# Attention and two dense products on one core: outputs and next scores as one piece in three PSUM banks

## The chip, the cores and the metric

The kernel runs on one core of a Trainium2 chip. The metric is the device time of one execution in microseconds (us). The kernel before takes 915.24 us, the median of three runs (914.27 to 915.32).

The core has a matrix engine (PE, whose weight loads are shown as PEld), a vector engine (DVE), a scalar engine (ACT), a third elementwise engine (POOL), and a queue (SP) that only issues DMAs here. Each engine works through its own list of instructions in order, and semaphores make one wait for another. PE writes its results to PSUM, a memory of eight banks; a bank holds 512 float32 values in each of 128 partitions. DVE and ACT read PSUM.

## The reference

For 8 batches of 8 heads, 576 positions and head size 64, masked attention is computed. Heads 0 to 3 look at the 32 latest positions, heads 4 to 7 at every fourth of the 128 latest. The result, 4608 rows of 512, goes through two dense products with an ELU between them:

```python
scores = np.where(masks, q @ k.T / sqrt(64), -1e9)
attn = softmax(scores)                       # per row, sum + 1e-9
x = (attn @ v) as (4608, 512)
h = x @ w_in                                 # (4608, 2048)
g = np.where(h > 0, h, np.exp(np.minimum(h, 0)) - 1)
out = g @ w_out                              # (4608, 512)
```

All is float32. The kernel gets near that accuracy with a faster matmul type (fp32r): it splits a value into a high part and a low part and forms three products (high times high, high times low, low times high).

## The kernel before, in words

**Tiling.** The 4608 rows are worked in nine chunks of 512 (`NCH`, index c), the 2048 hidden columns in 16 tiles of 128 (`NF`, index f). For each chunk and hidden tile, `product1` (L285) forms the first product in one PSUM bank `h_ps` with 12 matmuls; `elu` (L302) turns it into `gh` and `gl`; and `gemm2` (L318) adds 12 matmuls into four banks `o_ps`, the chunk's output. In the first 12 hidden tiles of chunk 0 the weights aren't split yet: there are four matmuls in full float32 in place of each 12.

**Order on PE.** All matmuls keep the order in which the program lists them (`mm`, L81). In the main loop (L403) hidden tile f runs its first product, then a step of attention if one is due, then the second product of tile f - 2 (`flush(LAG)`). After a chunk's last second product, `store` (L326) copies the four output banks with ACT and SP stores them.

**Order on the other engines.** The order on ACT, DVE, POOL and SP is made by a planner, which simulates the kernel's time and takes instructions as they become ready, those with the least slack first. `tc.issue_after(ins)` ties what is listed in the block behind `ins` on the same engine. So the order on ACT and DVE can't be read in the code; it can be read in the trace.

**Attention.** A pair is two heads; a batch has four pairs (`NPAIR`). The first batch goes through `first_attention` (L193) before chunk 0. During chunk c (0 to 6), `batch_attention(c + 1)` (L332) works the next batch in eight steps, spread over the hidden tiles (L432: f = 1, 3, 5, 7, 9, 11, 13, 14): scores of pair 0, scores of 1, outputs of 0, scores of 2, outputs of 1, scores of 3, outputs of 2, outputs of 3. Chunks 7 and 8 have no attention beside them.

A scores step (`attention` up to its first `yield`, L242 to L263) puts 36 small matmuls, 72 instructions, into the two banks `a_ps0` and `a_ps1` (`banks`, L189), 384 columns each. DVE adds the mask (L252), takes the row maxima (L253, L254); ACT takes 12 exponentials with their sums (L256); the sums are inverted, POOL multiplies (L183, in batch 1 DVE does), and DVE transposes into `pt` (L262). An outputs step (`outputs`, L163) has 12 matmuls of 96 columns, 24 instructions, into the same two banks, and two ACT copies of 288 columns into `x32` (L173, L176). At the start of a chunk `split_x` (L271) splits 512 rows of `x32` into `xh` and `xl`.

**PSUM in the main loop.** Four banks `o_ps`, two `a_ps`, two `h_ps` (the pool `ps_h`, bufs=2, L373): eight in all. A bank `h_ps` is read by ACT (L304, the exponential) and by DVE (L311, the maximum with zero); the next but one first product may write it after both.

**Loads.** `load_pair` (L147) has SP load the q, k and v of a pair into buffers of which there are two each. The weights come through `load_w` (L84); some rooms `early` (L67) serve the first batch before a weight tile takes them.

Of the kernel before, what the change touches and what calls it, by code (L numbers as in the profile page):

```python
# [10 lines left out]
F32 = mybir.dt.float32  # L11
# [12 lines left out]
P = 128  # L24
G = 32
# [21 lines left out]
def body(ctx: ExitStack, tc: tile.TileContext, q, k, v, masks, w_in, w_out, out):  # L47
# [141 lines left out]
    def banks():  # L189

        return [ps_a.tile([P, TC], F32, name=f"a_ps{i}") for i in range(2)]

    def first_attention(hp, loaded):  # L193

        dil = hp >= NPAIR // 2
        qt, kt, vt = loaded
        if hp >= 2:
            sm = early[2 * (hp - 2) + 1][:QB, 2 * NU * D:2 * NU * (D + 2 * G)].rearrange("p (u j) -> p u j", u=2 * NU)
        else:
            sm = ap.tile([QB, 2 * NU, 2 * G], F32, name="sm")  # L200
        mx = ap.tile([QB, 2 * NU], F32, name="nmx", bufs=4)
        sums = ap.tile([QB, 2 * NU], F32, name="sums", bufs=4)
        s_ps = ps_f.tile([P, 2, TC], F32, name="ab"[hp % 2])[:QB, :, :NU * 2 * G]
        for h in range(2):
            mm(s_ps[:, h, :], ones_sb, mask_sb[:, int(dil), :], start=True, stop=False)
        scores([s_ps[:, h, :] for h in range(2)], qt, kt, False)
        yield
        s4 = s_ps.rearrange("p h (n j) -> p h n j", n=NU)
        mx4 = mx.rearrange("p (h n) -> p h n", h=2)
        inorder(nc.vector.tensor_reduce(out=mx4, in_=s4, op=ALU.max, axis=mybir.AxisListType.X))  # L210
# [12 lines left out]

        t_ps = (ps_c, ps_f)[hp % 2].tile([P, 2, TC], F32, name="ca"[hp % 2])
        for n in range(NU):
            for h in range(2):
                o = n % NA * QB
                mm(t_ps[h * 2 * G:(h + 1) * 2 * G, n // NA, o:o + QB], sm[:, h * NU + n, :], ident, start=True, stop=True)
        t4 = t_ps[:, :, :NA * QB].rearrange("p i (n q) -> p i n q", n=NA)
        for h in range(2):  # L230
            to = tr[:, h * NU:(h + 1) * NU, :].rearrange("p (i n) q -> p i n q", i=2)
            for c, r, m in ((0, 0, 2), (1, 0, 1), (1, 1, 1), (2, 0, 2)):
                cs, ks, rs = slice(c * G, (c + 1) * G), slice((c + r) * G, (c + r + m) * G), slice((h * 2 + r) * G, (h * 2 + r + m) * G)
                if hp == NPAIR - 1:
                    inorder(nc.vector.tensor_copy(out=to[ks, :, :, cs], in_=t4[rs, :, :, cs]))
                else:
                    inorder(nc.scalar.copy(out=to[ks, :, :, cs], in_=t4[rs, :, :, cs]))
            yield
        a_ps = ps_f.tile([P, 2, TC], F32, name="db"[hp % 2])
        yield outputs(0, hp, [(a_ps[:, i, :], i * NA, (i + 1) * NA) for i in range(NU // NA)], vt, tr, inorder)  # L240

    def attention(b, hp, loaded):  # L242

        dil = hp >= NPAIR // 2
        qt, kt, vt = loaded
        sm = ap.tile([QB, 2 * NU, 2 * G], F32, name="sm")
        nmx = ap.tile([QB, 2 * NU], F32, name="nmx", bufs=4)
        sums = ap.tile([QB, 2 * NU], F32, name="sums", bufs=4)
        s_ps = [s[:QB, :NU * 2 * G] for s in banks()]
        scores(s_ps, qt, kt, True)  # L250
        for h in range(2):
            nc.vector.tensor_tensor(out=sm[:, h * NU:(h + 1) * NU, :].rearrange("p n j -> p (n j)"), in0=s_ps[h], in1=mask_sb[:, int(dil), :], op=ALU.add)  # L252
        nc.vector.tensor_reduce(out=nmx, in_=sm, op=ALU.max, axis=mybir.AxisListType.X)  # L253
        nc.vector.tensor_scalar(out=nmx, in0=nmx, scalar1=-0.125, scalar2=None, op0=ALU.mult)  # L254
        for u in range(2 * NU):
            nc.scalar.activation(out=sm[:, u, :], in_=sm[:, u, :], func=AF.Exp, bias=nmx[:, u:u + 1], scale=0.125, accum_out=sums[:, u:u + 1])  # L256
        normalise(nc.vector if b < 2 else nc.gpsimd, sm, sums, lambda ins: ins)
        tr = transposed()
        for c in range(GU):
            for r in range(2):  # L260
                ks, cs, rs = slice((c + r) * G, (c + r + 1) * G), slice(c * G, (c + 1) * G), slice(r * G, (r + 1) * G)
                nc.vector.transpose(out=tr[ks, :, cs], in_=sm[cs, :, rs])  # L262
        yield  # L263
        outputs(b, hp, [(a, i * NA, (i + 1) * NA) for i, a in enumerate(banks())], vt, tr)
        yield

    xh, xl = [None] * NC, [None] * NC

    hidden, below = [], []

    def split_x(c):  # L271
        for hp in range(NC):
# [11 lines left out]

    def product1(c, f):  # L285

        h_ps = ps_h.tile([P, TC], F32, name="h_ps")
        i = 2 * f
        if c == 0 and f < F0:
            terms = [(full[i], x32[0][:, n, :TC], n) for n in range(NC)]  # L290
        else:
            terms = [(wh[i], x[n], n) for n in range(NC) for x in (xh, xl)] + [(wl[i], xh[n], n) for n in range(NC)]
        for t, (w, x, n) in enumerate(terms):
            mm(h_ps, w[:, n * P:(n + 1) * P], x, start=t == 0, stop=t == len(terms) - 1)
            yield h_ps
# [5 lines left out]

    def elu(h_ps, first):  # L302
        e = fp.tile([P, TC], F32, name="e", bufs=3)
        nc.scalar.activation(out=e, in_=h_ps, func=AF.Exp)  # L304
        if first:
            below.append(nc.scalar.activation(out=e, in_=e, func=AF.Relu, scale=-1.0, bias=1.0).ins)
            g = fp.tile([P, TC], F32, name="gh", bufs=3)
            hidden.append(nc.vector.scalar_tensor_tensor(out=g, in0=h_ps, scalar=0.0, in1=e, op0=ALU.max, op1=ALU.subtract).ins)
            return g, None
        nc.vector.tensor_scalar(out=e, in0=e, scalar1=1.0, scalar2=-1.0, op0=ALU.min, op1=ALU.add)  # L310
        hidden.append(nc.vector.scalar_tensor_tensor(out=e, in0=h_ps, scalar=0.0, in1=e, op0=ALU.max, op1=ALU.add).ins)  # L311
        gh = fp.tile([P, TC], F32R, name="gh", bufs=3)
        gl = fp.tile([P, TC], F32R, name="gl", bufs=2)
        nc.scalar.copy(out=gh, in_=e)  # L314
        nc.vector.tensor_tensor(out=gl, in0=e, in1=gh.bitcast(F32), op=ALU.subtract)  # L315
        return gh, gl
# [15 lines left out]
    def batch_attention(b):  # L332

        x32[b] = xp.tile([P, NPAIR, S], F32, name="x32", bufs=2)

        old = None
        for hp in range(NPAIR):
            it = attention(b, hp, loaded.pop((b, hp)))
            next(it)
            nxt = b * NPAIR + hp + 1  # L340
            if nxt < B * NPAIR:
                loaded[divmod(nxt, NPAIR)] = load_pair(*divmod(nxt, NPAIR))
            yield
            if old is not None:
                next(old)
                yield
            old = it
        next(old)
        yield

    STEPS = 2 * NPAIR
    loaded = {}
    rooms = [room(0, hp) for hp in range(NPAIR)]

    for what in "m0 qk0 qk1 qk2 qk3 v0 v1 w0 v2 v3".split():
# [13 lines left out]
    for what in "S0 S1 M0 M1 S2 P0 M2 T0 U0 S3 P1 P2 A0 T1 M3 U1 O0 T2 U2 P3 B0 O1 T3 U3 O2 G0 G1 O3 G2 A1 C0 D1".split():  # L369
        i = int(what[1])  # L370
        if what == "G0":
            ps_second.close()
            ps_h = ctx.enter_context(tc.tile_pool(name="ps_h", bufs=2, space=bass.MemoryType.PSUM, side="right"))  # L373
            first = product1(0, 0)
        if what[0] == "A":
            inorder(magnitude(i))
# [10 lines left out]
    loaded[1, 0] = load_pair(1, 0)  # L387
    for j in range(NR - NE, NR + 2):
        load_w(j)
    split = 0  # L390
    pend = []
    o_of = {}

# [9 lines left out]
    for c in range(NCH):  # L403
# [2 lines left out]
                split_x(c)  # L406
        elif c > 1:
            split_x(c)
        att = batch_attention(c + 1) if c + 1 < B else iter(())
        emitted = 0  # L410
        for f in range(NF):
            while c == 0 and ready < min(NF, f + AHEAD):
# [13 lines left out]
            while c == 1 and split < min(K0, f + 2):  # L426
# [2 lines left out]
                    split_w(split)  # L429
                split += 1  # L430
            pend.append((c, f, elu(gemm1(c, f), c == 0 and f < F0)))
            while emitted < (f + 1) * STEPS // (NF - 1):  # L432
                emitted += 1
                if c == 0 and emitted <= 2:
# [65 lines left out]
```

## Time and profile before

| what | value |
|---|---|
| median of the three runs | 915.24 us (914.27 to 915.32) |
| the profiled execution, its own time | 914.69 us |
| its span, first to last instruction | 912.9 us |
| mean granted PE clock | 0.994 of full |
| PE busy | 895.5 us, 98% |
| PEld busy | 694.8 us, 76% |
| DVE busy | 530.6 us, 58% |
| ACT busy | 392.3 us, 43% |
| POOL busy | 45.0 us, 5% |
| idle time of PE that the wait table lists | 13.3 us, all before 131 us |

How to read it: rows of the timeline show start, duration, engine, line of the code, operation, `output<-inputs`, shapes and a count (x4) where equal neighbours are merged; in brackets stands idle time before them and what ended it. Large matmuls are pipelined, so their rows overlap (0.39 us long, one every 0.23 us); the pace is read from the starts. L82 is the helper through which every matmul goes, so matmuls are told apart by their tiles: `h_ps` first product, `o_ps` second product, `a_ps<-kt,qt` scores, `a_ps<-pt,vt` outputs. In a row of groups, `| 17.2, 584 |` is busy us and the mean of one in ns. In a row of stretches, `97.52 (x770)` is busy us and instructions of one engine.

### The profile page before, as it was taken

Reading aid. Unit: us, or ns where it says so; the run is one execution under the profiler, and the core shown is the slowest. Engines: PE = TensorE matmul, PEld = TensorE weight load, DVE = VectorE, ACT = ScalarE, POOL = GpSimd, SP = SyncE. Lnnn points to the kernel's source line nnn. Section 1 sums busy time; section 2 is a strip of 40 time slices with the busy share of each in tenths; the row PEclk is TensorE's granted clock in tenths of the full one; section 3 lists DMA queues with packets and bytes.
Section 4 is the critical chain, followed back from the end, with each engine's and each line's share of the span. In section 5 each row is a group of like instructions: output and inputs, shape, how many; then the busy total and the mean of one; then the engine's idle time right before and its main releaser. Section 6 shows DMA issues by size and latency. Waiting matters only on the chain.

```text
span 912.9 us, 15990 instructions
## 1 busy us (share of the span) xinstructions
PE 895.5 (98%) x6536; PEld 694.8 (76%) x6536; DVE 530.6 (58%) x926; ACT 392.3 (43%) x1185; POOL 45.0 (5%) x36
## 2 busy tenths in 40 slices
PE   6899989999999999999999999999999999999998
PEld 5444458888878887888888787888788888888886
DVE  5999998765465556554565556655655533343332
ACT  4763593543354434444543345433543432233222
POOL 2000000100001000000000001000000000000000
PEclk8999999999999999999999999999999999999999
DMA  9963102111031113101211112011300010001001
GB/s 350 404 233 121 44 19 81 54 46 34 29 101 45 45 36 101 43 23 60 73 45 45 46 46 88 29 45 36 101 19 18 1 47 1 0 1 47 1 1 46
DMA packets 23802, 59.40 MB, mean 65 GB/s; under 512 B 2640, under 2 KB 2736, under 8 KB 23728
## 3 DMA queue, kind: packets, MB, share of 16 engines
q1 hardware_dynamic: 23728, 58.37, 19.2%
q8 instruction: 51, 0.84, 0.4%
q14 instruction: 23, 0.19, 0.1%
HBM read 48.92 MB, written 9.44 MB: 64 GB/s over the span
## 4 chain that ended last, share of the span: by engine, by line
PE 87%; ACT 5%; DVE 4%; DMA 3%; issue 1%; SPq 0%; ACTq 0%; DVEq 0%
PE o_ps L82 41%; PE h_ps L82 40%; PE a_ps L82 5%; ACT sm L256 3%; DMA r<-w_out 2%; DMA r<-w_in 1%; ACT r L131 1%; DMA kt<-k 1%; DVE nmx L253 1%; DVE sm L252 1%; ACT e L304 0%; DVE a L115 0%; DVE a L113 0%; DVE e L311 0%; ACT o L329 0%
## 5 line engine op out<-in xcount | busy, mean ns | idle before, releaser
L82 PE MATMUL o_ps<-a,gh 128*128 128x512 f32 x576 | 207.3, 429 | 0.0
L82 PE MATMUL o_ps<-r,gh 128*128 128x512 f32 x576 | 195.3, 398 | 0.4
L82 PE MATMUL h_ps<-xh,r 128*128 128x512 f32 x512 | 183.5, 393 | 3.0 <-ACT x L173 3.0
L304 ACT ACTIVATE e<-h_ps 128x512 f32<-128x512 f32 x144 | 85.5, 594 | 228.6 <-PE h_ps L82 228.5
L314 ACT CAST gh<-e 128x512 fp32r<-128x512 f32 x132 | 82.0, 621 | 194.2 <-DVE e L311 194.1
L310 DVE TENSOR_SCALAR e<-e 128x512 f32<-128x512 f32 x132 | 63.5, 481 | 163.2 <-ACT e L304 162.1
L82 PE MATMUL h_ps<-xh,a 128*128 128x512 f32 x480 | 147.7, 389 | 0.0
L82 PE MATMUL h_ps<-xl,r 128*128 128x512 f32 x368 | 143.9, 391 | 0.0
L82 PE MATMUL o_ps<-r,gl 128*128 128x512 f32 x368 | 143.5, 390 | 0.0
L82 PEld LDWEIGHTS o_ps<-a,gh 128*128 128x128 f32 x576 | 106.5, 188 | 39.4 <-issue 19.6
L315 DVE TENSOR_TENSOR gl<-e,gh 128x512 fp32r<-128x512 f32 x132 | 91.2, 691 | 77.4 <-PE o_ps L82 60.1
L82 PEld LDWEIGHTS o_ps<-r,gh 128*128 128x128 f32 x576 | 106.6, 188 | 26.9 <-ACT o L329 2.5
L256 ACT ACTIVATE sm<-sm,nmx 96x64 f32<-96x64 f32 x336 | 112.1, 335 | 33.0 <-DVE nmx L254 32.6
L82 PEld LDWEIGHTS h_ps<-xh,r 128*128 128x128 f32 x512 | 96.7, 189 | 24.5 <-ACT x L173 3.8
L82 PEld LDWEIGHTS h_ps<-xh,a 128*128 128x128 f32 x480 | 90.1, 188 | 18.7
L262 DVE STREAM_TRANSPOSE pt<-sm 32x384 f32<-32x384 f32 x168 | 95.5, 568 | 12.9 <-POOL sm L183 11.0
L311 DVE SCALAR_TENSOR_TENSOR e<-h_ps,e 128x512 f32<-128x512 f32 x132 | 91.1, 690 | 4.0
L82 PEld LDWEIGHTS h_ps<-xl,r 128*128 128x128 f32 x368 | 69.6, 189 | 15.0 <-issue 0.5
L82 PEld LDWEIGHTS o_ps<-r,gl 128*128 128x128 f32 x368 | 69.1, 188 | 15.1
L183 POOL TENSOR_TENSOR sm<-sm,sums 96x768 f32<-96x768 f32 x25 | 40.4, 1616 | 654.8 <-ACT e L304 298.3
L256 ACT ACTIVATION_READ_ACCUMULATOR sm<-sm,nmx 96x1 f32 x336 | 62.9, 187 | 0.0
L82 PE MATMUL o_ps<-a,gl 128*128 128x512 f32 x160 | 62.5, 391 | 0.0
(90 smaller groups left out, 697.3 us busy)
## 6 DMA issues: line engine op xcount, KB each, us to landing
vt<-v SPq DMA_DIRECT2D x30, 384.0 KB, 3.0
kt<-k SPq DMA_DIRECT2D x30, 304.0 KB, 4.1
qt<-q SPq DMA_DIRECT2D x30, 288.0 KB, 3.2
r<-w_in SPq DMA_DIRECT2D x16, 512.0 KB, 7.7
r<-w_out SPq DMA_DIRECT2D x16, 512.0 KB, 7.8
out<-o SPq DMA_DIRECT2D x32, 256.0 KB, 3.4
out<-xl SPq DMA_DIRECT2D x4, 256.0 KB, 2.1
r<-v SPq DMA_DIRECT2D x2, 384.0 KB, 9.1
```

What stands on the lines that cost most here:

```text
L82: inorder(nc.tensor.matmul(*args, **kw))
L131: nc.scalar.copy(out=h, in_=full2[k])
L183: return keep(eng.tensor_tensor(out=sm, in0=sm, in1=sums.unsqueeze(2).broadcast_to([QB, 2 * NU, 2 * G]), op=ALU.mult))
L252: nc.vector.tensor_tensor(out=sm[:, h * NU:(h + 1) * NU, :].rearrange("p n j -> p (n j)"), in0=s_ps[h], in1=mask_sb[:, int(dil), :], op=AL ...
L253: nc.vector.tensor_reduce(out=nmx, in_=sm, op=ALU.max, axis=mybir.AxisListType.X)
L256: nc.scalar.activation(out=sm[:, u, :], in_=sm[:, u, :], func=AF.Exp, bias=nmx[:, u:u + 1], scale=0.125, accum_out=sums[:, u:u + 1])
L262: nc.vector.transpose(out=tr[ks, :, cs], in_=sm[cs, :, rs])
L304: nc.scalar.activation(out=e, in_=h_ps, func=AF.Exp)
L310: nc.vector.tensor_scalar(out=e, in0=e, scalar1=1.0, scalar2=-1.0, op0=ALU.min, op1=ALU.add)
L311: hidden.append(nc.vector.scalar_tensor_tensor(out=e, in0=h_ps, scalar=0.0, in1=e, op0=ALU.max, op1=ALU.add).ins)
L314: nc.scalar.copy(out=gh, in_=e)
L315: nc.vector.tensor_tensor(out=gl, in0=e, in1=gh.bitcast(F32), op=ALU.subtract)
```

## The change

In chunk 0 nothing moves: its batch keeps the steps of before (the function that makes them is now `probabilities`, which ends with the transposed probabilities; the outputs are called beside it). In chunks 1 to 6 attention goes in pieces (`piece`): the outputs of one pair and the scores of the next, with nothing between them on PE. They stand behind the first product of f = 0, 4, 7, 11 and 14 in chunk 1 and f = 2, 6, 10 and 14 in chunks 2 to 6. Chunk 1's first piece is scores alone; its last one holds the scores of the next batch's first pair; chunk 6's last piece is outputs alone.

A piece uses three banks: `a_ps0`, `a_ps1` and `h1`. The last 96 columns of the outputs go to `a_ps0`, behind the room of its scores, the other 480 to `h1`. ACT copies both out. The scores of the next pair go to the first 384 columns of `a_ps0` and `a_ps1`.

`h1` was one of the two banks of the first product. In chunks 1 to 6 the first product has only `h0`; in chunks 0, 7 and 8 it still alternates. After chunk 0's first 12 hidden tiles, ACT first copies the first product into SBUF (`h`, one buffer), and the exponential and DVE's maximum read the copy.

Of the 12 exponentials of a pair, six are listed with the piece, six and all that follows them after the next hidden tile's copy (`issue_after(freed[-1])`). The loads of the next pair are listed after the transposes. The buffer `sm` becomes a single one; in the first batch, pair 1's `sm` goes to a room of `early`.

```diff
-        if hp >= 2:
-            sm = early[2 * (hp - 2) + 1][:QB, 2 * NU * D:2 * NU * (D + 2 * G)]...
+        if hp > 0:
+            room, o = (early[0], WINDOW + 2 * S) if hp == 1 else (early[2 * (hp - 2) + 1], 2 * NU * D)
+            sm = room[:QB, o:o + 2 * NU * 2 * G].rearrange("p (u j) -> p u j", u=2 * NU)
...
-    def attention(b, hp, loaded):
+    def probabilities(b, hp, loaded, s_ps):
...
-        sm = ap.tile([QB, 2 * NU, 2 * G], F32, name="sm")
+        sm = ap.tile([QB, 2 * NU, 2 * G], F32, name="sm", bufs=1)
...
         for u in range(2 * NU):
+            if u == NU:
+                yield
             nc.scalar.activation(out=sm[:, u, :], in_=sm[:, u, :], func=AF.Exp, bias=nmx[:, u:u + 1], scale=0.125, accum_out=sums[:, u:u + 1])
...
-        yield
-        outputs(b, hp, [(a, i * NA, (i + 1) * NA) for i, a in enumerate(banks())], vt, tr)
-        yield
+        nxt = b * NPAIR + hp + 1
+        if nxt < B * NPAIR:
+            loaded_pairs[divmod(nxt, NPAIR)] = load_pair(*divmod(nxt, NPAIR))
+        yield b, hp, vt, tr
+
+    def piece(old, new):
+        a = banks()
+        if old is not None:
+            b, hp, vt, tr = old
+            if hp == 0:
+                x32[b] = xp.tile([P, NPAIR, S], F32, name="x32", bufs=2)
+            outputs(b, hp, [(a[0][:, NU * 2 * G:], NU - 1, NU), (ps_h.tile([P, TC], F32, name="h1"), 0, NU - 1)], vt, tr)
+        if new is None:
+            return None
+        steps = probabilities(*new, loaded_pairs.pop(new), a)
+        next(steps)
+        return steps
...
-        h_ps = ps_h.tile([P, TC], F32, name="h_ps")
+        h_ps = ps_h.tile([P, TC], F32, name=f"h{0 if 0 < c < B - 1 else f % 2}")
...
+        if not first:
+            h = fp.tile([P, TC], F32, name="h", bufs=1)
+            freed.append(nc.scalar.copy(out=h, in_=h_ps).ins)
+            h_ps = h
         nc.scalar.activation(out=e, in_=h_ps, func=AF.Exp)
...
-        att = batch_attention(c + 1) if c + 1 < B else iter(())
+        att = batch_attention(c + 1) if c == 0 else iter(())
+
+        when = () if c == 0 or c >= B - 1 else (0, 4, 7, 11, 14) if c == 1 else (2, 6, 10, 14)
...
             pend.append((c, f, elu(gemm1(c, f), c == 0 and f < F0)))
+            if steps is not None:
+                with tc.issue_after(freed[-1]):
+                    current, steps = next(steps), None
+            if f in when:
+                n = (c + 1) * NPAIR + when.index(f) + NPAIR + 1 - len(when)
+                current, steps = None, piece(current, divmod(n, NPAIR) if n < B * NPAIR else None)
```

More of the change, by code (lines that the diff above doesn't have):

```diff
@@ L196, in first_attention @@
         qt, kt, vt = loaded
-        if hp >= 2:
-            sm = early[2 * (hp - 2) + 1][:QB, 2 * NU * D:2 * NU * (D + 2 * G)].rearrange("p (u j) -> p u j", u=2 * NU)
+        if hp > 0:
+            room, o = (early[0], WINDOW + 2 * S) if hp == 1 else (early[2 * (hp - 2) + 1], 2 * NU * D)
+            sm = room[:QB, o:o + 2 * NU * 2 * G].rearrange("p (u j) -> p u j", u=2 * NU)
         else:
-            sm = ap.tile([QB, 2 * NU, 2 * G], F32, name="sm")
+            sm = ap.tile([QB, 2 * NU, 2 * G], F32, name="sm", bufs=1)
         mx = ap.tile([QB, 2 * NU], F32, name="nmx", bufs=4)
@@ L240, in first_attention @@
         yield outputs(0, hp, [(a_ps[:, i, :], i * NA, (i + 1) * NA) for i in range(NU // NA)], vt, tr, inorder)
-    def attention(b, hp, loaded):
+    def probabilities(b, hp, loaded, s_ps):
         dil = hp >= NPAIR // 2
         qt, kt, vt = loaded
-        sm = ap.tile([QB, 2 * NU, 2 * G], F32, name="sm")
+        sm = ap.tile([QB, 2 * NU, 2 * G], F32, name="sm", bufs=1)
         nmx = ap.tile([QB, 2 * NU], F32, name="nmx", bufs=4)
         sums = ap.tile([QB, 2 * NU], F32, name="sums", bufs=4)
-        s_ps = [s[:QB, :NU * 2 * G] for s in banks()]
+        s_ps = [s[:QB, :NU * 2 * G] for s in s_ps]
         scores(s_ps, qt, kt, True)
@@ L262, in attention @@
                 nc.vector.transpose(out=tr[ks, :, cs], in_=sm[cs, :, rs])
-        yield
-        outputs(b, hp, [(a, i * NA, (i + 1) * NA) for i, a in enumerate(banks())], vt, tr)
-        yield
+        nxt = b * NPAIR + hp + 1
[14 more added lines that the diff above has]
+        return steps
     xh, xl = [None] * NC, [None] * NC
     hidden, below = [], []
+    freed = []
     def split_x(c):
@@ L337, in batch_attention @@
         for hp in range(NPAIR):
[L338 to L342, printed above, removed]
+            *_, new = probabilities(b, hp, loaded_pairs.pop((b, hp)), banks())
             yield
             if old is not None:
-                next(old)
+                outputs(*old[:2], [(a, i * NA, (i + 1) * NA) for i, a in enumerate(banks())], *old[2:])
                 yield
-            old = it
-        next(old)
+            old = new
+        outputs(*old[:2], [(a, i * NA, (i + 1) * NA) for i, a in enumerate(banks())], *old[2:])
         yield
     STEPS = 2 * NPAIR
-    loaded = {}
+    loaded_pairs = {}
     rooms = [room(0, hp) for hp in range(NPAIR)]
@@ L372, in body @@
             ps_second.close()
-            ps_h = ctx.enter_context(tc.tile_pool(name="ps_h", bufs=2, space=bass.MemoryType.PSUM, side="right"))
+            ps_h = ctx.enter_context(tc.tile_pool(name="ps_h", bufs=1, space=bass.MemoryType.PSUM, side="right"))
             first = product1(0, 0)
@@ L386, in body @@
     ps_a = ctx.enter_context(tc.tile_pool(name="ps_a", bufs=1, space=bass.MemoryType.PSUM))
-    loaded[1, 0] = load_pair(1, 0)
+    loaded_pairs[1, 0] = load_pair(1, 0)
     for j in range(NR - NE, NR + 2):
@@ L390, in body @@
     split = 0
+    current = steps = None
     pend = []
```

## The prediction, made before the result was known

> I call the scores of a head pair S, its outputs O, the hidden tile index f, the chunk index c, and the two matmul products of a hidden tile first and second product. T is the moment at which O starts on PE.
>
> **What bounds the kernel now.** I read the page first: the engine table, the slices, the shares of the chain.
>
> ```profile
> span 912.9 us, 15990 instructions
> ...
> PE 895.5 (98%) x6536; PEld 694.8 (76%) x6536; DVE 530.6 (58%) x926; ACT 392.3 (43%) x1185; POOL 45.0 (5%) x36
> ...
> DVE  5999998765465556554565556655655533343332
> ...
> PEclk8999999999999999999999999999999999999999
> ...
> PE 87%; ACT 5%; DVE 4%; DMA 3%; issue 1%; SPq 0%; ACTq 0%; DVEq 0%
> ```
>
> PE is the bound at full clock. DVE is full only in slices 2 to 6 (23 to 137 us, chunk 0 with the weight conversion). But a busy PE is not a PE at its pace, so next come stages: a whole chunk with attention, one stretch without, and a hole in chunk 0.
>
> ```profile
> 127.40:130.60 3.20, 0.19 (x2) 0.11 (x1) 3.13 (x6) 3.20 (x6) 0.00 (x0) 0.91 0.00 0
> 130.60:133.60 3.00, 3.00 (x8) 2.38 (x9) 3.00 (x4) 2.54 (x4) 0.00 (x0) 0.53 0.00 0
> ...
> 444.95:542.55 97.60, 97.52 (x770) 78.70 (x769) 55.05 (x104) 42.68 (x148) 6.39 (x4) 1.00 0.18 53
> ```
>
> ```profile
> 745.00:832.00 87.00, 87.00 (x386) 72.06 (x385) 31.26 (x53) 23.68 (x40) 0.00 (x0) 1.00 0.03 13
> ```
>
> Columns are the stretch, its length, then busy time and count for PE, weight loads, DVE, ACT, POOL, then granted clock. Without attention 87.00 us hold some 384 whole large matmuls (386 with those cut by the edges), 0.2266 us each; so 16 hidden tiles of 24 matmuls cost 87.0 us. A chunk with attention costs 97.60 us, so four S, four O and whatever stalls cost 10.6 us, 2.65 us per pair. ACT is busy 42.7 of 97.6 us there and DVE 55.
>
> Next, what one S and one O take of PE (timeline of PE around one of each):
>
> ```profile
> 309.76 1.07 PE L82 MATMUL h_ps<-xh,a 128*128 128x512 f32 x4
> 310.76 0.97 PE L82 MATMUL a_ps<-kt,qt 64*32 64x64 f32 x72
> 311.65 0.72 PE L82 MATMUL o_ps<-a,gh 128*128 128x512 f32 x2
> 312.22 0.40 PE L82 MATMUL o_ps<-a,gl 128*128 128x512 f32 x1
> ...
> 321.78 1.07 PE L82 MATMUL h_ps<-xh,r 128*128 128x512 f32 x4
> 322.78 1.21 PE L82 MATMUL a_ps<-pt,vt 128*64 128x96 f32 x24
> 323.92 0.74 PE L82 MATMUL o_ps<-r,gh 128*128 128x512 f32 x2
> 324.50 0.40 PE L82 MATMUL o_ps<-r,gl 128*128 128x512 f32 x1
> ```
>
> Four matmuls from 309.76 would let the next start at 309.76 + 4 x 0.2266 = 310.67; S starts at 310.76, so the way in costs 0.09. S itself takes 311.65 - 310.76 = 0.89. The two large matmuls behind it take 312.22 - 311.65 = 0.57 in place of 0.45, so the way out costs 0.12. O: 0.09, 1.14 and 0.13. The weight loads say why: usually they run one matmul ahead, at each change of shape they do not.
>
> ```profile
> 309.53 0.87 PEld L82 LDWEIGHTS h_ps<-xh,a 128*128 128x128 f32 x4
> 310.75 0.81 PEld L82 LDWEIGHTS a_ps<-kt,qt 64*32 64x32 f32 x72 [0.35 <-issue]
> ```
>
> So S costs 1.10 and O 1.36, 2.46 together and 9.84 in a chunk; 0.76 of the 10.6 is left for stalls and slower spacing.
>
> **The change, part by part.**
>
> *One piece in place of two.* A joint piece enters once and leaves once: it saves one way in and one way out, 0.09 + 0.12 = 0.21. From O (128x64) to S (64x32) the shape still changes; the pause that S needs is the one at the end of O, which I already count inside its 1.14. Chunk 1 has five pieces (its first S alone), chunks 2 to 6 four each (the last O alone): 25 pieces, 23 of them joint. 23 x 0.21 = **-4.8 us**. Bounds: 0 (the change of shape in the middle costs what both ways did) and 0.35 each, the whole pause of the weight loads, -8.1. I take 0.21, since it is measured at exactly these edges.
>
> The 0.35 pause stands at every change of shape. The Trainium skill, "TensorEngine Tiling (Array Packing)", Tiling Modes, Key Properties, says that changing the tiling mode drains TensorE while another tile of the same mode does not; by it three of four drains stay in a joint piece, which speaks against hoping for half. That would be one drain per joint piece, which the trace prices no higher than the way in and out above.
>
> *S moves from f = 1 and 3 to f = 2, 6, 10, 14 (chunks 2 to 6).* Before, the exponentials of the first S lie in ACT's order ahead of the last copy that empties the output banks:
>
> ```profile
> 453.25 0.39 PE L82 MATMUL o_ps<-r,gl 128*128 128x512 f32 x1
> 453.72 0.50 PE L82 MATMUL o_ps<-r,gh 128*128 128x512 f32 x1
> 454.05 0.39 PE L82 MATMUL o_ps<-a,gh 128*128 128x512 f32 x1
> ```
>
> ```profile
> 453.01 0.19 ACT L256 ACTIVATION_READ_ACCUMULATOR sm<-sm,nmx 96x1 f32 x1
> 453.11 0.56 ACT L329 COPY o<-o_ps 128x512 f32<-128x512 f32 x1
> ```
>
> The wait table does not list it, but PE loses 0.47 - 0.23 and then 0.33 - 0.23, 0.34 us, in each such chunk. With S at f = 2 no exponentials are due before those copies, which have the whole first product of f = 2 (2.7 us). Five chunks: **-1.7**. Bounds 0 and -1.7.
>
> *Copying the first product out (ACT).* 132 tiles get one more ACT copy. The copy of an output bank has the same shape; ACT's rows at one O show where it goes:
>
> ```profile
> L329 ACT COPY o<-o_ps 128x512 f32<-128x512 f32 x32 | 17.2, 584 | 1.4 <-PE o_ps L82 1.1
> ...
> L173 ACT COPY x<-a_ps 128x288 f32<-128x288 f32 x28 | 11.0, 400 | 1.2
> ```
>
> ```profile
> 427.22 1.21 PE L82 MATMUL a_ps<-pt,vt 128*64 128x96 f32 x24
> ```
>
> ```profile
> 427.39 0.60 ACT L304 ACTIVATE e<-h_ps 128x512 f32<-128x512 f32 x1 [2.56 <-PE h_ps L82]
> 427.99 0.89 ACT L173 COPY x<-a_ps 128x288 f32<-128x288 f32 x2
> ...
> 433.50 1.95 ACT L281 CAST xh<-x 128x256 fp32r<-128x256 f32 x6 [3.67 <-PE h_ps L82]
> 435.35 0.59 ACT L304 ACTIVATE e<-h_ps 128x512 f32<-128x512 f32 x1
> ```
>
> 132 x 0.584 = 77 us raises ACT from 392 to 469 of 913: no bound. The exponential and DVE's max then read SBUF; the cast of that size reads SBUF in like time, so 0. In chunks 1 to 6 there is one bank, so the next first product waits for the copy. With O starting at 427.22, ACT takes up the first product at 427.39, at T + 0.17. Copy done at 0.17 + 0.58 = 0.75, and a hand-over (0.15 below) makes 0.9 us, against 12 x 0.227 = 2.7 us of second product: 1.8 us of cover. Without cover ACT must be held longer than that. Its longest train there was twelve exponentials:
>
> ```profile
> 510.11 0.35 ACT L256 ACTIVATE sm<-sm,nmx 96x64 f32<-96x64 f32 x1 [1.55 <-DVE nmx L254]
> ...
> 514.12 0.58 ACT L304 ACTIVATE e<-h_ps 128x512 f32<-128x512 f32 x1
> ```
>
> 4.0 us; the change cuts it into two halves of 2.0 with the copy of the next tile between them (the second half is tied behind it). Queued behind the waiting copy are that tile's exponential, the cast, then DVE's work. One SBUF buffer h adds that a copy waits for the DVE max of the tile before, 2.0 us after its product of a 5.4 us period. I take **+1.0 us** for late copies in all; bounds 0 and 0.2 at each of 24 S (2.0 + 0.9 - 2.7), +4.8.
>
> *S in the bank that O has just used.* O's last 96 columns lie in the first scores bank beside S's 384. ACT must read them before S may write that bank, and PE waits in order, with S, the second product and the next first product behind it. The copy of the hidden tile holds ACT until T + 0.75; 96 columns take 0.400 - 192 x (0.584 - 0.400)/224 = 0.24 by the two copy rows, so T + 0.99, with the hand-over T + 1.14. O is through at T + 1.14. Nothing to spare: I take 0.05 in 23 pieces, **+1.2**; bounds 0 and +0.6 each (below, the first rival).
>
> *Chunk 0's hole.* The first product of f = 14 waits for a bank that DVE still reads:
>
> ```profile
> 130.52 0.77 PE L82 MATMUL h_ps<-xh,r 128*128 128x512 f32 x1 [3.01 <-ACT x L173]
> ```
>
> ```profile
> 126.18 3.47 DVE L262 STREAM_TRANSPOSE pt<-sm 32x384 f32<-32x384 f32 x6
> 129.68 0.69 DVE L311 SCALAR_TENSOR_TENSOR e<-h_ps,e 128x512 f32<-128x512 f32 x1
> ...
> 134.03 0.68 DVE L315 TENSOR_TENSOR gl<-e,gh 128x512 fp32r<-128x512 f32 x1
> ```
>
> The profile names an ACT copy; but the max of f = 12 (two banks, two tiles back) ends at 130.37, 0.15 before PE starts. PE idles 3.0 and then runs at clock 0.53 for 3.0 us, six or seven matmuls at 0.2266/0.53 = 0.43: 1.4 more. An ACT copy frees the bank before; its exponential sat at 124.37 in ACT's order, in time for 127.5. The stall does not vanish: the second product of f = 12 would start at about 127.5 + 2.7 + 1.4 = 131.6 and needs gl, which DVE, full here, ends at 134.71 in its present order. From there ten of twelve matmuls, 137.0, against 138.8 now: **-1.5** after 0.3 for four more copies on an ACT that is full too. Bounds: -4.4 (all of it) and +1.0.
>
> *Hidden.* The pair's three loads are issued later, on SP's queue, with two to three hidden tiles (11 to 16 us) to land; the slowest of them takes 4.1.
>
> ```profile
> kt<-k SPq DMA_DIRECT2D x30, 304.0 KB, 4.1
> ```
> Moving one first-stage buffer into a weight room delays one weight load until that pair is transposed; that weight is converted by a DVE that is full until then. Both 0, up to +1.
>
> Sum on the profile's own time, 912.9 span + 1.8 around it = 914.69: 914.7 - 4.8 - 1.7 + 1.0 + 1.2 - 1.5 = 908.9. The median, 915.24, is 0.55 above the profiled execution, so 908.9 to 909.4; I say 909.0.
>
> **The rivals.**
>
> *The small copy comes second (the other side).* If ACT's order has the exponential (0.60) between the tile's copy and the 96-column copy, S starts at T + 1.74, and PE stands 0.6 in 23 pieces in place of 0.05: 909.0 + 23 x 0.55 = 921.7. Without any such wait the forecast is 909.0 - 1.2 = 907.8, 7.4 under the median of before, so from 7.4/23 = 0.32 per piece on the change loses. For it: in the row at 427.39 the exponential goes before the copies of O. Against: those copies were ready later and no one waited for them at once; six casts for which PE does wait (433.50) went ahead of an exponential (435.35) at a chunk's start. The Trainium skill, "PSUM — Partial Sum Buffer", PSUM bank collisions, tells one to guard by bank and quadrant rather than by address; by it S has to wait although no column is shared. No row of before can show that.
>
> *The single bank is late.* Copies always behind six exponentials: +4.8 in place of +1.0, 912.8; more where chunk starts crowd ACT.
>
> *No gain in the middle.* The change of shape inside the piece costs both ways: 909.0 + 4.8 = 913.8.
>
> *The hole closes.* DVE's order shifts with it: 909.0 - 2.9 = 906.1.
>
> **How the numbers follow.** The forecast (906.5 to 912) 0.50; hole closes 0.13; single bank late 0.12; no gain in the middle 0.10; small copy second 0.15. A measurement of this kernel can tell about 0.2%, 1.8 us: faster is below 913.4, slower above 917.1. Faster 0.50 + 0.13 + 0.07 + 0.02 = 0.72; same 0.05 + 0.07 = 0.12; slower the rest, 0.16. The range 904.5 to 917.0 leaves out the small copy's case and the far end of the hole. The likeliest's own range is 906.5 to 912.
>
> **What would show it.** A stretch of one chunk (2 to 5) at 96.4 us or less plus waits; main matmuls resuming 2.2 to 2.3 us after O starts; S beginning 1.15 after O, with no idle PE before it (0.6 there is the first rival); ACT in the order copy, 96-column copy, exponential; no pause at the fourth output bank; the first product starting 0.227 after the second product's last matmul (a gap there is the single bank). The forecast is wrong if chunks 2 to 5 take over 97.2 us, or if chunk 0 ends later than now.

## The result, and the profile after

| kernel | median | lowest and highest | ratio to before, 95% interval |
|---|---|---|---|
| before | 915.28 us | 914.27 to 915.51 | |
| after | 922.12 us | 921.04 to 923.16 | 1.0078, 1.0064 to 1.0092 |

Four runs of each stand behind the table. The change makes the kernel slower by 0.8%. The forecast was 909.0 us, faster by 0.7%, with a range of 904.5 to 917.0. The sign was wrong and the time lies outside the range.

The span grew from 912.9 to 919.3 us. From the page of the kernel after, the answers to the first lines shown of before:

```profile
span 919.3 us, 16120 instructions
...
PE 889.4 (97%) x6536; PEld 694.0 (75%) x6536; DVE 553.1 (60%) x926; ACT 463.2 (50%) x1317; POOL 45.9 (5%) x36
...
PE 77%; DVE 10%; ACT 6%; DMA 3%; issue 2%; SPq 1%; DVEq 0%; ACTq 0%
```

PE is busy 6.1 us less than before (895.5), as a saving should look, and yet the span is 6.4 us longer: PE waits more. The chain of waits shows for whom, with DVE up from 4% to 10%.

Where on the way is the time lost? A landmark that all kernels have is the start of the outputs at f = 14. First the timeline of PE before, then after: these rows are in chunks 0, 1 and 6 (the counts are cut by the window asked for).

```profile
134.81 0.63 PE L82 MATMUL a_ps<-pt,vt 128*64 128x96 f32 x10
...
232.00 0.54 PE L82 MATMUL a_ps<-pt,vt 128*64 128x96 f32 x7
...
720.02 0.47 PE L82 MATMUL a_ps<-pt,vt 128*64 128x96 f32 x6
```

```profile
130.26 1.21 PE L82 MATMUL a_ps<-pt,vt 128*64 128x96 f32 x24 [0.20 <-ACT x L173]
...
232.11 0.39 PE L82 MATMUL a_ps<-pt,vt 128*64 128x96 f32 x4
...
726.36 0.39 PE L82 MATMUL a_ps<-pt,vt 128*64 128x96 f32 x4
```

Chunk 0 gains 4.55 us up to its outputs. From there to chunk 1's, 4.66 are lost again (101.85 for 97.19). From there to chunk 6's, five chunks lose 6.23 (494.25 for 488.02), where the forecast had its gain. These three make 6.34 of the 6.4.

The table of stretches of the kernel after (stretch, length, then busy time and count of PE, PEld, DVE, ACT, POOL; clock; DMA share) cuts at the starts of pieces: an ordinary piece with four hidden tiles, the one across the start of a chunk, and the whole chunk behind it.

```profile
357.75:381.80 24.05, 24.05 (x193) 19.77 (x192) 14.08 (x24) 11.63 (x38) 1.68 (x1) 1.00 0.14 43
429.92:456.54 26.62, 24.64 (x193) 19.69 (x192) 16.66 (x32) 16.11 (x50) 1.47 (x1) 1.00 0.22 77
456.54:555.34 98.80, 96.79 (x769) 79.01 (x768) 58.99 (x104) 51.01 (x164) 6.62 (x4) 1.00 0.17 52
```

An ordinary stretch is 24.05 us and PE has no gap in it. The one across a chunk start does the same work and takes 26.62, 2.57 more. Four at 24.05 are 96.20; the chunk takes 98.80. So the whole loss of a chunk is one place, and it comes five times (chunks 2 to 6; chunk 6 ends without scores, so none follows it).

At that place, the timeline of PE, from the piece at f = 14 to the next piece:

```profile
429.92 0.39 PE L82 MATMUL a_ps<-pt,vt 128*64 128x96 f32 x4
...
431.06 0.97 PE L82 MATMUL a_ps<-kt,qt 64*32 64x64 f32 x72
431.96 0.74 PE L82 MATMUL o_ps<-r,gh 128*128 128x512 f32 x2
...
442.69 0.49 PE L82 MATMUL h<-xh,r 128*128 128x512 f32 x1 [0.87 <-ACT xh L302]
444.28 0.50 PE L82 MATMUL h<-xl,r 128*128 128x512 f32 x1 [1.10 <-DVE xl L303]
```

The piece itself goes as forecast: the scores start 1.14 after the outputs and no gap stands before them. Some 11 us later the next chunk's first product waits twice, 0.87 for the high part of x and 1.10 for the low part. ACT's timeline there, from the piece on:

```profile
430.08 0.58 ACT L328 COPY h<-h 128x512 f32<-128x512 f32 x1 [2.04 <-PE h L82]
430.56 0.24 ACT L173 COPY x<-a_ps 128x96 f32<-128x96 f32 x1
430.69 0.64 ACT L330 ACTIVATE e<-h 128x512 f32<-128x512 f32 x1
...
437.09 1.95 ACT L302 CAST xh<-x 128x256 fp32r<-128x256 f32 x6 [0.26 <-PE h L82]
438.94 0.57 ACT L328 COPY h<-h 128x512 f32<-128x512 f32 x1
439.42 0.35 ACT L259 ACTIVATE sm<-sm,nmx 96x64 f32<-96x64 f32 x1
...
441.42 0.39 ACT L302 CAST xh<-x 128x256 fp32r<-128x256 f32 x1
441.71 0.62 ACT L330 ACTIVATE e<-h 128x512 f32<-128x512 f32 x1
442.24 0.39 ACT L302 CAST xh<-x 128x256 fp32r<-128x256 f32 x1
```

The reader sees copy, 96-column copy, exponential, in the order that the forecast needed. Then six of the eight casts of x; the copy of f = 15; behind it the second half of the exponentials, 2.0 us from 439.42 to 441.42; and only then cast 7, the tile's own exponential and cast 8. PE's pause ends at 442.69, 0.06 after the last cast (442.24 + 0.39). DVE and POOL next:

```profile
442.37 1.52 DVE L336 TENSOR_SCALAR e<-e 128x512 f32<-128x512 f32 x1
443.81 0.41 DVE L303 TENSOR_TENSOR xl<-x,xh 128x256 fp32r<-128x256 f32 x1
```

```profile
442.14 1.47 POOL L183 TENSOR_TENSOR sm<-sm,sums 96x768 f32<-96x768 f32 x1 [23.49 <-DVE sums L182]
```

DVE's row L336 has a median of 0.427 us over its 132 instances; here it takes 1.52, while POOL multiplies, and the last low part of x stands behind it. It ends at 444.22, and PE goes on at 444.28. The first pause is thus ACT's order, the second seems to be DVE held up beside POOL. PE's wait table adds up the five chunk starts (waits in total, times, longest):

```profile
PE h L82 <- DVE xl L303: 5.8, 5, 1.2
PE h L82 <- ACT xh L302: 4.4, 5, 0.9
```

Together 10.2 of the 12.85 us (5 x 2.57). A listed wait counts from the end of the row before (0.39 us), while at full pace the next matmul starts after 0.23, so some 0.16 of each pause is not in it; and behind a pause the next start comes after 0.34. Chunk 1's loss has rows of its own, of the same timeline of PE:

```profile
131.82 0.73 PE L82 MATMUL o_ps<-r,gh 128*128 128x512 f32 x2 [0.35 <-ACT gh L340]
134.04 0.50 PE L82 MATMUL o_ps<-r,gl 128*128 128x512 f32 x1 [1.49 <-DVE gl L341]
...
158.22 0.50 PE L82 MATMUL o_ps<-r,gh 128*128 128x512 f32 x1 [1.29 <-ACT o L355]
...
167.77 0.50 PE L82 MATMUL h<-xh,r 128*128 128x512 f32 x1 [1.08 <-ACT h L328]
```

The first two stand at the end of chunk 0: the late `gl` that the forecast saw behind the closed hole. The third is the output copy behind exponentials (the piece at f = 0). The fourth is the single bank. They list 4.2 us; with the 0.16 ahead of each and the 0.11 behind it that are not listed, some 5.3, against some 0.6 that three joint pieces save. That is about the 4.66 (each of the two stretches holds four scores steps, 288 matmuls).

### The profile page after: what moved, and what is told of

Read it like the earlier page. It is cut to its first block, busy times and chain, and to the rows that moved or that the text cites. A ratio compares the mean times of both kernels' runs of the same rounds, so it can differ in the third digit from the quotient of the medians.

```text
span 919.3 us, 16120 instructions
## 1 busy us (share of the span) xinstructions
PE 889.4 (97%) x6536; PEld 694.0 (75%) x6536; DVE 553.1 (60%) x926; ACT 463.2 (50%) x1317; POOL 45.9 (5%) x36
## 4 chain that ended last, share of the span: by engine, by line
PE 77%; DVE 10%; ACT 6%; DMA 3%; issue 2%; SPq 1%; DVEq 0%; ACTq 0%
PE h L82 38%; PE o_ps L82 36%; PE a_ps L82 3%; ACT sm L259 2%; DMA r<-w_out 2%; DVE a L115 1%; ACT xh L302 1%; DVE a L113 1%; DVE e L336 1%; ACT r L131 1%; DMA kt<-k 1%; DVE a L110 1%; DVE pt L265 1%; DMA vt<-v 1%; DVE a L112 1%
## 5 line engine op out<-in xcount | busy, mean ns | idle before, releaser
L82 PE MATMUL o_ps<-r,gh 128*128 128x512 f32 x576 | 193.1, 394 | 1.6 <-ACT o L355 1.3
L82 PE MATMUL h<-xh,r 128*128 128x512 f32 x512 | 183.6, 393 | 5.5 <-ACT xh L302 4.4
L336 DVE TENSOR_SCALAR e<-e 128x512 f32<-128x512 f32 x132 | 62.8, 475 | 161.8 <-ACT e L330 159.7
L82 PE MATMUL h<-xl,r 128*128 128x512 f32 x368 | 143.9, 391 | 5.8 <-DVE xl L303 5.8
L82 PE MATMUL h<-xh,a 128*128 128x512 f32 x480 | 147.8, 389 | 0.0
L328 ACT COPY h<-h 128x512 f32<-128x512 f32 x132 | 77.1, 584 | 133.2 <-PE h L82 133.2
L82 PEld LDWEIGHTS h<-xh,r 128*128 128x128 f32 x512 | 96.1, 188 | 28.4 <-ACT xh L302 6.5
L337 DVE SCALAR_TENSOR_TENSOR e<-h,e 128x512 f32<-128x512 f32 x132 | 112.0, 849 | 4.3
L82 PEld LDWEIGHTS h<-xh,a 128*128 128x128 f32 x480 | 90.1, 188 | 18.7
L330 ACT ACTIVATE e<-h 128x512 f32<-128x512 f32 x144 | 90.4, 628 | 21.2 <-PE h L82 18.7
L82 PEld LDWEIGHTS h<-xl,r 128*128 128x128 f32 x368 | 69.1, 188 | 22.4 <-DVE xl L303 7.7
```

The lines of the kernel that those rows point to most:

```text
L82: inorder(nc.tensor.matmul(*args, **kw))
L328: freed.append(nc.scalar.copy(out=h, in_=h_ps).ins)
```

## The experiments

The theory to be tried: the loss is the tail of the piece at f = 14 (second half of the exponentials, POOL's multiply, DVE's transposes) meeting the split of x for the next chunk, and without that meeting the kernel takes what was forecast. The rivals: the copy on ACT costs it, the single bank costs it, or the pieces themselves do.

### The tail behind the next chunk's first copy

One condition keeps the second half of the exponentials of the f = 14 piece back until the copy of f = 0 of the next chunk.

```diff
-            if steps is not None:
+            if steps is not None and f < NF - 1:
```

> One tie is changed: the second half of a piece at f = 14 is listed behind the next chunk's first copy in place of the copy of f = 15. Positions on PE, copies, banks as in the changed kernel. A: the pauses go, 909.3, a chunk 96.3 us; perhaps 0.5 more if the next outputs (f = 2) then wait for their transposes. B: the copy of f = 15 is as late as before, so 916 or more. C: 919 or more.

Measured: 909.44 us (909.05 to 909.74), ratio 0.9938 (0.9924 to 0.9953). A whole chunk of it, from the table of stretches, and ACT's timeline at the chunk start:

```profile
330.52:426.80 96.28, 96.25 (x770) 79.10 (x768) 59.33 (x104) 50.79 (x165) 6.72 (x4) 1.00 0.17 54
```

```profile
434.65 0.58 ACT L328 COPY h<-h 128x512 f32<-128x512 f32 x1
435.12 0.71 ACT L302 CAST xh<-x 128x256 fp32r<-128x256 f32 x2
...
439.46 0.35 ACT L259 ACTIVATE sm<-sm,nmx 96x64 f32<-96x64 f32 x1
```

Casts 7 and 8 now follow the copy at once, the exponentials start 4.8 us behind that copy, not 0.5, and PE has no pause at any chunk start. The chunk takes 96.28, 2.52 less than after. Cast 8 also goes ahead of the tile's own exponential here; the planner made that order. One condition moves the time by 12.7 us, five times 2.5. That settles the place of the loss: neither the copy nor the single bank nor the pieces.

### All pieces one tile earlier

If the tail's meeting with the split is the loss, moving the pieces should take it away as well.

```diff
-        when = () if ... else (0, 4, 7, 11, 14) if c == 1 else (2, 6, 10, 14)
+        when = () if ... else (0, 4, 7, 11, 14) if c == 1 else (1, 5, 9, 13)
```

> The pieces of chunks 2 to 6 stand one hidden tile earlier (f = 1, 5, 9, 13), so the second six exponentials of the last piece fall at f = 14 and no longer beside the next chunk's split of x; the single bank, the copies and the joint pieces stay. Theory A (the second six exponentials stand in ACT's order between the casts of the next chunk's xh, and PE waits for the last casts): the 2.57 us pauses at five chunk starts go, 922.1 - 5 x 2.57 = 909.3, a chunk 96.3 us. Theory B (the copy out of the single bank is what comes late at chunk starts): the pauses stay to more than half, 916 or more. Theory C (joint pieces cost more than single ones): 919 or more.

Measured: 926.07 us (925.23 to 926.92), ratio 1.0120 (1.0105 to 1.0136). A miss: it got slower still. DVE's timeline at the same chunk start, then PE's, then the stretch behind it and the one behind the next chunk start (the clock is the third number from the end):

```profile
439.17 1.84 DVE L337 SCALAR_TENSOR_TENSOR e<-h,e 128x512 f32<-128x512 f32 x1
440.94 3.47 DVE L265 STREAM_TRANSPOSE pt<-sm 32x384 f32<-32x384 f32 x6
...
445.05 2.76 DVE L303 TENSOR_TENSOR xl<-x,xh 128x256 fp32r<-128x256 f32 x8
```

```profile
444.04 0.49 PE L82 MATMUL h<-xh,r 128*128 128x512 f32 x1 [0.41 <-ACT h L328]
445.86 0.69 PE L82 MATMUL h<-xl,r 128*128 128x512 f32 x1 [1.32 <-DVE xl L303]
```

```profile
446.30:449.50 3.20, 3.20 (x9) 2.39 (x8) 2.54 (x7) 0.59 (x1) 0.00 (x0) 0.51 0.02 5
...
546.00:549.40 3.40, 3.40 (x13) 2.02 (x14) 2.85 (x8) 0.48 (x1) 0.00 (x0) 1.00 0.02 5
```

The exponentials are out of the way, but now the end of the tail meets the split: DVE's maximum is stretched to 1.84 beside POOL, six transposes follow, and all eight low parts of x stand behind them. After the pauses PE runs at a granted clock of 0.51 for some 3 us. The pauses alone do not bring this: it happens behind three of the five chunk starts of this execution, and not behind the one at 545.87, though the pauses there are the same 0.41 and 1.32. So "exponentials ahead of the casts" was too narrow; it is the whole tail, and each engine's part of it arrives at another time.

With chunk 1 moved too, (1, 4, 7, 10, 13):

> As the first run, and chunk 1's pieces at f = 1, 4, 7, 10, 13 in place of 0, 4, 7, 11, 14. Chunk 1 lost 1.29 to the emptying of the output banks behind six exponentials and 1.08 to a late copy, both behind its first piece at f = 0. If that early piece is the cause, both go: 909.3 - 2.4 = 907. If DVE's weight splits are the cause wherever the piece stands, 909 as the first run.

Measured: 923.98 us (923.75 to 926.60), ratio 1.0104 (1.0088 to 1.0120). That is 2.1 us less, with the same pieces in the other chunks: a miss for the same reason. In chunk 1 the wait for the output copy and the 1.08 for the late copy are gone, as expected, but PE now waits 1.31 before the outputs at 171.52. At all five later chunk starts stand the same pauses of 0.4 and 1.3 (here the clock stays full behind each).

### The pieces at f = 0, 4, 8 and 12

Three tiles between the last piece and the split, in place of two or one.

```diff
+        when = () if ... else (0, 3, 6, 9, 12) if c == 1 else (0, 4, 8, 12)
```

> The tie as in the changed kernel; pieces at f = 0, 4, 8, 12 (chunk 1: 0, 3, 6, 9, 12). The last piece's tail, some 16 us from the start of its outputs to the last transpose, ends before the split of x begins (10.9 us later for the second half's copy, 16.3 for the chunk's end). Theory A widened (no part of the tail, neither exponentials on ACT nor transposes on DVE, may meet the split): no pause at chunk starts, 909.3; the piece at f = 0 puts exponentials ahead of the output copies as before, which may cost back 0.3 to 1.3 in six chunks: 909 to 917. If the pauses come from the single bank: 920 as before.

Measured: 912.98 us (911.92 to 913.63), ratio 0.9980 (0.9971 to 0.9990). The long pauses at the chunk starts are gone, and a chunk takes 96.67 (250.37 to 347.04). That is 0.4 over the 96.28 above, and PE's timeline shows where: at 342.95, the first matmul of the new chunk waits for the copy of f = 15, which ACT ends at 342.90, behind six casts of x. It starts some 0.3 late, and the next one 0.1 more; the same stands at all five chunk starts. In chunk 1 PE waits 2.0 before the outputs at 167.18 and 1.3 for an output copy. So distance ahead of the split helps as well, at a price elsewhere: the single bank, late by a little at each chunk start, and chunk 1.

### No halves

All 12 exponentials in one train, with no tie.

```diff
-            if u == NU:
-                yield
...
-                with tc.issue_after(freed[-1]):
-                    current, steps = next(steps), None
```

> The changed kernel with all twelve exponentials listed with the piece (no half behind the next copy). What is tested: is the tie of the second half to the copy of f = 15 all that hurts, or any attention work beside the split of x? If only the tie: 909.5 as with the later half. If any work of the pair's tail there hurts (twelve exponentials end 1.6 later than six, then POOL and the transposes meet the split): pauses of 0.6 to 2.5 at five chunk starts stay, 912 to 922. Rival on the single bank: a copy behind twelve exponentials, 4.0 us, comes too late at every piece, 24 x 0.5 to 1: 921 or more; by the rows the copy would be done 9.5 us after the outputs start and is needed at 10.5, so I expect no pause there.

Measured: 941.73 us (940.85 to 943.00), ratio 1.0300 (1.0282 to 1.0317), beyond every expectation. DVE's timeline and PE's at the chunk start (the line numbers of this kernel are smaller by two or three):

```profile
448.07 3.00 DVE L300 TENSOR_TENSOR xl<-x,xh 128x256 fp32r<-128x256 f32 x5
451.00 3.47 DVE L263 STREAM_TRANSPOSE pt<-sm 32x384 f32<-32x384 f32 x6
454.50 1.10 DVE L300 TENSOR_TENSOR xl<-x,xh 128x256 fp32r<-128x256 f32 x3
```

```profile
454.99 0.72 PE L82 MATMUL h<-xl,r 128*128 128x512 f32 x1 [3.46 <-DVE xl L300]
```

Here the transposes come right in the middle of the split, and PE stands 3.46 us at one go; after it the clock is 0.52 for 3 us. But at an ordinary piece PE loses nothing, though ACT has 12 exponentials in one train: the rival "the single bank is late" falls there. In this kernel the halves are worth 20 us, nearly all of it at the chunk starts, where the low clock adds to the pauses.

### The copy alone

The kernel before with nothing but ACT's copy of the first product, still in two banks, with the room for `sm` that it needs.

```diff
+        if not first:
+            h = fp.tile([P, TC], F32, name="h", bufs=1)
+            nc.scalar.copy(out=h, in_=h_ps)
+            h_ps = h
```

> The kernel before with only ACT's copy of the first product (two banks, scores and outputs apart as before; one buffer sm, for room). A: the copy costs nothing where two banks stand behind it and closes the hole in chunk 0 as in the changed kernel (its f = 14 outputs start at 130.3 in place of 134.8, some 2.3 of the 4.5 are lost again to DVE): 915.3 - 2.3 = 913, chunks 2 to 6 at 97.6 us. B: half a microsecond more of ACT at each chunk start makes PE wait there too: chunks of 98 us or more, 916 to 919.

Measured: 912.88 us (911.30 to 913.20), ratio 0.9971 (0.9959 to 0.9984). As expected: the copy costs nothing and closes chunk 0's hole (its outputs start at 130.47, before at 134.81). A chunk takes 97.43. The whole kernel gains 2.3, of which five chunks at 97.43 instead of 97.60 are 0.85; so 1.45 of the 4.34 is kept.

### POOL's part, by two runs

First the multiply goes to DVE for all batches, on the kernel with the tail held back.

```diff
-        normalise(nc.vector if b < 2 else nc.gpsimd, sm, sums, lambda ins: ins)
+        normalise(nc.vector, sm, sums, lambda ins: ins)
```

> The later half as in the second run, with the multiplication of the probabilities on DVE (0.95 us) in place of POOL (1.66 us). What is tested is a cost by itself: in the changed kernel single rows of DVE's add and max took 1.5 to 1.85 us in place of 0.43 and 0.69, where POOL multiplies. If POOL's work is the cause, no row of them is above 0.75 us here. The time: same as the second run within 1 us, since PE waits for none of it there.

Measured: 939.37 us (939.13 to 939.47), ratio 1.0270 (1.0255 to 1.0286). The stretched rows are gone: the longest L336 is 0.428 us, the longest L337 0.695. But the time is far off, for another reason. DVE's timeline in an ordinary piece, then ACT's, then PE's:

```profile
375.83 2.89 DVE L265 STREAM_TRANSPOSE pt<-sm 32x384 f32<-32x384 f32 x5
378.75 0.69 DVE L337 SCALAR_TENSOR_TENSOR e<-h,e 128x512 f32<-128x512 f32 x1
```

```profile
379.48 0.62 ACT L340 CAST gh<-e 128x512 fp32r<-128x512 f32 x1 [4.83 <-DVE e L337]
380.00 0.58 ACT L328 COPY h<-h 128x512 f32<-128x512 f32 x1
```

```profile
380.64 0.50 PE L82 MATMUL h<-xh,r 128*128 128x512 f32 x1 [1.03 <-ACT h L328]
```

With the multiply on DVE the planner puts five transposes ahead of the maximum. The maximum holds the one buffer `h` and the cast; the next copy stands behind that cast; the single bank stays full; PE waits 1.03 us. It happens at each of 24 pieces, 24.6 us in the wait table. This run does not say what POOL costs, but it shows the single bank late, through DVE's order and not through exponentials.

So the second run keeps the order. It is the kernel after, and POOL divides only one of 12 blocks in the five pairs of f = 14; a tie keeps the transposes in their place. The rows of PE, ACT and DVE stand in the same order in both traces.

```diff
-        normalise(nc.vector if b < 2 else nc.gpsimd, sm, sums, lambda ins: ins)
+        n = 2 * NU if hp > 0 or b < 3 else 1
+        normalise(nc.vector if b < 2 else nc.gpsimd, sm[:, -n:, :], sums[:, -n:], lambda ins: ins)
...
-                nc.vector.transpose(out=tr[ks, :, cs], in_=sm[cs, :, rs])
+                with tc.issue_after(hidden[-1] if n == 1 else hidden[0]): nc.vector.transpose(...)
```

> The changed kernel, but in the five pairs whose piece stands at f = 14 (the ones that meet the next chunk's split of x) GpSimd divides one block of 64 columns out of twelve, so the other eleven stay undivided in those pairs. The order on TensorE, ScalarE and VectorE is the one of the changed kernel. Theory: the 2.57 us lost at each of five chunk starts are two things, six exponentials ahead of ScalarE's last casts (the pause of 0.87) and VectorE's row stretched from 0.43 to 1.52 while GpSimd multiplies (the pause of 1.10). Then the second pause goes to 0.1 or less, the first stays at 0.87, a chunk start loses about 1.4, and the time is 922.1 - 5 x 1.1 = 916.6. Rival: GpSimd's multiply only happens to lie beside it and VectorE is late for another reason; then both pauses stay and the time stays at 922.

Measured: 915.54 us (914.70 to 916.48), ratio 0.9998 (0.9988 to 1.0008). PE and DVE at the chunk start:

```profile
440.88 0.50 PE L82 MATMUL h<-xh,r 128*128 128x512 f32 x1 [0.89 <-ACT xh L302]
441.38 0.50 PE L82 MATMUL h<-xl,r 128*128 128x512 f32 x1
```

```profile
440.56 0.43 DVE L336 TENSOR_SCALAR e<-e 128x512 f32<-128x512 f32 x1
```

The row is back at 0.43, the second pause is gone, the first is what it was. The stretch across the chunk start is 25.49 (428.14 to 453.63), 1.44 over the ordinary one; 1.4 was expected. So of the 2.57, 1.13 came through POOL's multiply beside DVE, and 1.44 is left with the exponentials in ACT's order. The time fell by 6.6 us, 1.1 more than 5 x 1.1; the four runs of the kernel after differ by 2.1 us among themselves.

### A version that beats both

On the kernel with the tail held back, chunk 1's pieces leave f = 0, where the exponentials met the output copies:

```diff
-        when = () if ... else (0, 4, 7, 11, 14) if c == 1 else (2, 6, 10, 14)
+        when = () if ... else (1, 5, 8, 11, 14) if c == 1 else (2, 6, 10, 14)
```

> The later half as in the second run, and chunk 1's pieces at f = 1, 5, 8, 11, 14. The second run keeps two pauses in chunk 1, 0.35 (the output banks' emptying behind exponentials) and 1.10 (a copy behind a cast that waits for DVE's transposes). If the piece at f = 0 is their cause: 909.4 - 1.5 = 908. If DVE's weight splits are, 909.4.

Measured: 907.52 us (906.87 to 908.89), ratio 0.9924 (0.9909 to 0.9939). The wait for the output copy is gone from chunk 1, the one for the single bank is 0.89. The waits explain less than the 1.9 us: the profiled execution of the kernel with the tail held back also ran 3.41 us at a clock of 0.50 at the end of chunk 0 (134.62 to 138.03), which costs 1.7, and the one of this kernel did not, though its pauses there are the same (0.35 and 1.49).

## Why the prediction was wrong, by its own steps

**The step that failed** is "Copying the first product out", where the exponentials are cut into two halves with "the second half tied behind" the next tile's copy. The halves were priced against one thing only, the single bank: 2.0 us of train against 1.8 of cover. What the tie does at f = 14 was not asked. There the next tile is f = 15, and behind its copy ACT has the last casts of the next chunk's x, for which PE does wait. The prediction even quotes those casts as work for which PE waits, in its first rival, and did not put the moved exponentials beside them; the rival of the late bank says "more where chunk starts crowd ACT" and gives that no price. The missing term is 5 x 2.57 = 12.85 us; by the run with the short multiply, 1.44 of each 2.57 is the exponentials ahead of the casts, and 1.13 is POOL's multiply beside DVE, which the tie brought to the same place and which no term of the prediction names. Holding the tail back gives 909.44, where the forecast said 909.0 without it; the near match is partly luck, as the steps below show.

**A second miss in the same step** is that the maximum "then read[s] SBUF", priced at 0. It is no longer the same row: before, its input came from PSUM and its longest instance was 0.694 us. From the table of groups, before and then after (busy us, mean ns):

```profile
L311 DVE SCALAR_TENSOR_TENSOR e<-h_ps,e 128x512 f32<-128x512 f32 x132 | 91.1, 690 | 4.0
```

```profile
L337 DVE SCALAR_TENSOR_TENSOR e<-h,e 128x512 f32<-128x512 f32 x132 | 112.0, 849 | 4.3
```

That is 21 us more on DVE. It is 18 rows of 132: those beside POOL's multiply take 1.84 to 1.85 each, the other 114 at most 0.694. Before, with the input in PSUM, 17 rows lay beside the multiply and none took more than 0.694. The cost is hidden nearly everywhere; with the pieces one tile earlier it is the 1.84 at the head of the loss. The Trainium skill, "SBUF — State Buffer", Who interferes with whom and Summary, states it: a DVE instruction with two SBUF inputs contends with a GpSimd instruction that reads SBUF, and the later one blocks until the first is through. The rows agree: all 18 start 0.38 to 0.39 after the multiply and end 0.55 after its end.

**One piece in place of two, -4.8, with the S in O's bank, +1.2.** Right. Per piece the forecast had 2.46 - 0.21 + 0.05 = 2.30; measured is 24.05 less 96 matmuls of 0.2266, 2.30. The scores started 1.14 after the outputs, without a gap, so the 0.05 was rather 0 (the next item says what took its place); "no gain in the middle" and "the small copy comes second" both fall. That the latter gives 921.7, close to the 922.12 measured, is chance: the order on ACT was the forecast's. Two readings beside the sum were off. Main matmuls resumed 2.04 after the outputs (429.92 to 431.96), not 2.2 to 2.3; the prediction's own rows, 1.14 + 0.89, give 2.03. And the 0.35 pause of the weight loads is not at every change of shape: in both kernels it stands where small matmuls follow large ones, while from outputs to scores the loads are 0.1 apart.

**S moved away from f = 1 and 3, -1.7.** Right in sign. A chunk without the loss takes 96.28 and before took 97.60, so 1.32 less, where the steps give 0.34 + 4 x 0.16 = 0.98. The 0.76 that the forecast left for stalls and spacing fell to 0.08 (9.28 for four pieces at 2.30), that is by 0.68 and not by 0.34. The other 0.34 is the slower spacing. In the kernel before, each of the eight steps takes 0.04 to 0.07 more, from its start to the next step's, than the prediction's rows give (the stall of 0.34 aside; scores of pair 1 to outputs of pair 0, 457.34 to 469.36: 12.02 for 48 x 0.2266 + 1.10 = 11.98), 0.42 in a chunk. Four joint pieces have 0.05 each of it, inside their 2.30, and the chunk 0.08 beside.

**The single bank, +1.0.** One listed pause of 1.08 in all, in chunk 1, and none at the other pieces. The size is right; its mechanism differs from the forecast's train of exponentials: ACT's row before the late copy is the cast, as in the run with the multiply on DVE. With the pieces moved ahead, the bank was late at the chunk starts too, behind six casts (0.41 with the pieces one tile earlier).

**Chunk 0's hole, -1.5.** The hole closed by 4.55 at the outputs, and `gl` then came late by 1.49 as foreseen. The copy alone keeps 1.45 of it, so the size is right. Whether the clock falls behind that late `gl` differs between executions: the profiled ones of the copy alone and of the kernel with the tail held back have 3.41 us at 0.50 there, the one of the changed kernel none; the forecast had no term for it. "The hole closes", for all its 4.4, falls.

**Chunk 1** was not worked by itself: the output copy behind the piece at f = 0 (1.29) was missed, though the same wait at f = 1 was priced for chunks 2 to 6. With the tail held back that wait was 0.35, and removing it and 0.2 of the single bank's came with 1.9 us, most of which is the clock at the end of chunk 0 in the executions profiled.

**Hidden.** The loads and the room, 0: PE's waits show no load of a pair after chunk 0. Right.

The forecast's own sign of failure, a chunk over 97.2, came out: 98.80.

## What to carry to other kernels

When a change moves work on an engine that is half idle, look for the one place in the loop where that engine is on the critical path, here the split at the chunk start, and lay the moved work beside it tile by tile; a mean load of 50% says nothing there. Follow the moved work to its end, too: each of exponentials, multiply and transposes collided at another offset, so moving it by one tile only changed the collider, and what helped was to take all of it clear of the split, behind it (909.44) or three tiles ahead of it (912.98). A tie that is right at an ordinary tile should be tried at the first and last tile of the loop before it is priced.

## What the runs showed of the hardware

A multiply of 96 x 768 on POOL held up DVE rows of 128 x 512 beside it: 0.43 to 1.52 us (one input, in SBUF) and 0.69 to 1.84 (two). With the same order and a short multiply the former was 0.43 again. It was there before the change too, on the row with one input (longest 1.699 us), where PE's wait table listed nothing for it. What decides is which starts first. In the kernel after, 18 of the one-input rows began 0.07 us ahead of a multiply and took 0.43; the 6 that began behind its start all ended 0.28 to 0.29 after its end.

The clock can fall after short pauses, and the length of the pauses alone does not decide it. With the pieces one tile earlier, pauses of 0.41 and 1.32 us were followed by 3.2 us at 0.51; two chunk starts of the same execution, with the same pauses, were followed by full clock, and so were all five when chunk 1 was moved too. In the kernel after, 0.87 and 1.10 were followed by full clock. The Trainium skill, "TensorE: Matmul & The Clock Gate", What's actually happening, puts the fall after an idle window of about 3.4 us; the trace does not agree with that as a length of pause. In the trace's clock records each of these falls lasts 3.41 us, and they start at 248.03, 347.02 and 446.01, each 29 x 3.413 after the one before. What decided whether a pause cost the clock is open.
